# Dense backward of a four-layer attention stack: full-row band products, the feature map's derivative on VectorE, transposes moved behind the dh products

## The chip, the cores and the metric

The kernel runs on one core of one Trainium2 chip. The metric is the device time of one execution, in microseconds, as the median of several runs. Five engines take part: TensorE (PE in the profile, with PEld for its weight loads), VectorE (DVE), ScalarE (ACT), GpSimd (POOL) and SyncE (SP), which issues most of the transfers. Sixteen DMA engines move the data.

## The reference

Four residual layers run on 2048 rows of 640 numbers, 32 heads of 20 each. Layers 0 and 2 (kind A) are linear attention, layers 1 and 3 (kind B) are softmax attention in a sliding window of 256. The kernel computes the output and the gradients of the input and of the four weight matrices. The two parts that matter here are these:

```python
phi = lambda t: jnp.where(t > 0, t + 1, jnp.exp(t)) + 1e-6      # kind A
pq, pk = phi(q), phi(k)
kv = jnp.einsum("bhsd,bhse->bhde", pk, v)
z = jnp.einsum("bhsd->bhd", pk)
num = jnp.einsum("bhqd,bhde->bhqe", pq, kv)
den = jnp.einsum("bhqd,bhd->bhq", pq, z)[..., None] + 1e-6
o = num / den
...
x = x + _A_ref(_layernorm(x), A_wqkv, A_wo)      # layer 0, and again layer 2
x = x + _B_ref(_layernorm(x), B_wqkv, B_wo)      # layer 1, and again layer 3
```

The derivative of `phi` follows from its saved value: it is min(phi - 1e-6, 1). The kernel calls it `dphi`.

## The kernel before

The program does the forward pass, then for l = 3 and l = 1: the attention backward of layer l, and `seg_dense_bwd(l)`. The latter takes the gradient through the projection and the layer norm of layer l, and through the whole of layer a = l - 1 of kind A. It has two loops over 16 tiles of 128 rows. In loop 1 the gradient `dh` of the layer norm's output is the product of `dqkvT` (15 blocks of 128) with `WT`, in two halves of 320 columns (15 matmuls each, `dh0` and `dh1`). `ln_bwd` makes `car` of it, the gradient that flows on:

```python
def flip(self, src, n, dst, pt, eng, first=0):          # transposes on TensorE, up to 8 blocks per PSUM tile
    for i0 in range(0, n, 8):
        k = min(8, n - i0)
        tp = pt.tile([P, 1024], BF, name="t")
        for i in range(k):
            nc.tensor.transpose(tp[:, i * P:(i + 1) * P], src[:, c:c + P], self.ident)   # line 690
        (eng[(i0 // 8) % len(eng)])(dst[:, i0:i0 + k, :], v)                             # line 692

def ln_bwd(self, l, tt, ps, hn, g, pw):
    nc.scalar.activation(dhs, ps, ACT.Copy, scale=rs, accum_out=sm[:, 0:1])              # dh_s
    nc.vector.tensor_tensor_reduce(out=junk, in0=dhs, in1=hn, ..., accum_out=sm[:, 1:2]) # dh_junk
    nc.vector.tensor_scalar_mul(ab, sm, -1.0 / D)                                        # dh_ab
    nc.vector.scalar_tensor_tensor(out=u, in0=hn, scalar=ab[:, 1:2], in1=dhs, ...)       # dh_u
    nc.vector.scalar_tensor_tensor(out=self.car[:, tt, :], in0=u, scalar=ab[:, 0:1], in1=g, ...)
...
# seg_dense_bwd, loop 1
def flip_g(t):       # transposes car (5 blocks) into gT, copied by ScalarE; car is stored
def dO(t):
    p = self.do_mm(gT.pop(t), WoTA, pps)                     # 10 matmuls
    dN[t] = p1w.tile([P, 6 * P], BF, name="dN", bufs=3)
    s = self.do_scaled(a, t, p, o.pop(t), dN[t][:, 0:D], p1w)   # VectorE: dN; GpSimd: do_o; VectorE: do_s
    nc.gpsimd.memset(dN[t][:, D + H:], 0.0)
    nc.vector.tensor_copy(dN[t][:, D:D + H], s)
def flip_dN(t):      # transposes dN (6 blocks) into dNT, copied by ScalarE
def dq_band(t):
    for c in range(2):
        nc.tensor.matmul(p[:, c, 0:HD], lhsT=w[0:H, 5, :], rhs=mbdT[0:H, 5, ...])        # 32 rows, line 1075
        self.band_mm(p[:, c, 0:HD], w, mbdT, c, True)        # 3 narrow matmuls each, line 762
    ...                                                      # 10 matmuls into the bands, line 1083
    nc.gpsimd.tensor_scalar(out=f, in0=q, scalar1=-1e-6, scalar2=1.0, op0=ALU.add, op1=ALU.min)   # dphi
    nc.vector.tensor_tensor(out=dq[t], in0=p, in1=f, op=ALU.mult)
def flip_dq(t):      # transposes dq (5 blocks) into dqT, copied by ScalarE
plan = ((fetch, 2), (dh0, 0), (flip_g, -1), (flip_dN, -2), (dh1, 0), (dO, -1), (dq_band, -2), (flip_dq, -3))
for s in range(-2, TT + 3):
    for f, d in plan:
        if 0 <= s + d < TT:
            f(s + d)
```

The accumulators `d` of loop 1 rotate over two tiles of PSUM, the transposes `t` over two as well. Loop 2 has the same shape for the keys and values of layer a. `dkdv` makes two band products (with a one-row matmul of ones, line 1135) and multiplies the first by `dphi`; `flip_dkv` transposes 10 blocks, eight copied by ScalarE and two by VectorE; `dh0`/`dh1` and `ln_bwd` give the next `car`. Where a > 0 (so for l = 3 alone) `flip_g`, `dO` and `flip_dO` prepare the next attention backward. Its accumulators rotate over three tiles. An engine executes its instructions in order; the order between the steps of a loop is set by a scheduler when the program is built, from the order of the plan.

In the attention backward of layer 1 the weight gradients of layers 3 and 2 are filled in, so many pieces (a matmul or a load) per step; when they are done, the weights `WT`, `WoT` and `mbdT` of the dense part are put in the queue of loads, two per step, and the rest in one go at the end:

```python
self.seg_attention_bwd(l, it, lambda s: 11.9)     # 11.9 pieces per step
self.drain(it)
```

Of the kernel before, what the change touches and what calls it, by code (L numbers as in the profile page):

```python
# [12 lines left out]
ALU = mybir.AluOpType  # L13
# [3 lines left out]
P = 128  # L17
# [6 lines left out]
class Kern:  # L24
# [654 lines left out]
        self.dma(tile, dram, self.nc.sync)  # L679
        return tile  # L680

    def flip(self, src, n, dst, pt, eng, first=0):

        nc = self.nc
        for i0 in range(0, n, 8):
            k = min(8, n - i0)
            tp = pt.tile([P, 1024], BF, name="t")
            for i in range(k):
                c = (first + i0 + i) * P
                nc.tensor.transpose(tp[:, i * P:(i + 1) * P], src[:, c:c + P], self.ident)  # L690
            v = tp[:, 0:k * P].rearrange("p (i q) -> p i q", q=P)
            (eng[(i0 // 8) % len(eng)])(dst[:, i0:i0 + k, :], v)  # L692

    def do_mm(self, gT, WoT, pps):
        ps = pps.tile([P, 2, 512], F32, name="d")
# [30 lines left out]
        nc.vector.tensor_sub(sl[:, :, DH + 1], s, sl[:, :, DH])  # L726
        self.store(self.sv[l]["dO"][:, tt, :], dO)

    def dh_mm(self, ps, c, parts, WT):

        lhs = [t[:, k, :] for t, n in parts for k in range(n)]
        for k, w in enumerate(lhs):
            self.nc.tensor.matmul(ps[:, c, 0:self.HD], lhsT=w, rhs=WT[:, k, c * self.HD:(c + 1) * self.HD],  # L733
                                  start=(k == 0), stop=(k == len(lhs) - 1))

    def ln_bwd(self, l, tt, ps, hn, g, pw):
# [12 lines left out]
        nc.vector.scalar_tensor_tensor(out=u, in0=hn, scalar=ab[:, 1:2], in1=dhs, op0=ALU.mult, op1=ALU.add)  # L749
        nc.vector.scalar_tensor_tensor(out=self.car[:, tt, :], in0=u, scalar=ab[:, 0:1], in1=g,  # L750
                                       op0=ALU.add, op1=ALU.add)

    def dphi(self, p, pw):

        self.nc.gpsimd.tensor_scalar(out=p, in0=p, scalar1=-1e-6, scalar2=1.0, op0=ALU.add, op1=ALU.min)

    def band_mm(self, ps, lhsT, mat, c, seen):

# [254 lines left out]
    def seg_dense_bwd(self, l, w, mid):  # L1013
# [5 lines left out]
        with ExitStack() as st:  # L1019
# [7 lines left out]
            with ExitStack() as s2:  # L1027
                p1 = self.pool(s2, "b1")
                p1w = self.pool(s2, "b1w", 2)
                pl = self.pool(s2, "b1l", 3)  # L1030
                WTB, WoTA, mbdT = w
                WTA = WoTB = None
                pps = self.pool(s2, "ps", 2, PSUM)
                pbd = self.pool(s2, "psb", 1, PSUM)
                bands = [pbd.tile([P, 512], F32, name=f"band{i}") for i in range(2)]
                seen = [False, False]
                dT, hn, g, o, pq, ps, gT, dN, dNT, dq = ({} for _ in range(10))

# [12 lines left out]
                def dh1(t):  # L1051
                    self.dh_mm(ps[t], 1, [(dT.pop(t), self.QTT)], WTB)
                    self.ln_bwd(l, t, ps.pop(t), hn.pop(t), g.pop(t), pw)

                def flip_g(t):
                    gT[t] = pw.tile([P, DT, P], BF, name="gT")
                    self.flip(self.car[:, t, :], DT, gT[t], pt, [nc.scalar.copy])
                    self.dma(self.g_d[a][:, t, :], self.car[:, t, :], nc.gpsimd)

                def dO(t):  # L1060
                    p = self.do_mm(gT.pop(t), WoTA, pps)
                    dN[t] = p1w.tile([P, 6 * P], BF, name="dN", bufs=3)
                    s = self.do_scaled(a, t, p, o.pop(t), dN[t][:, 0:D], p1w)
                    nc.gpsimd.memset(dN[t][:, D + H:], 0.0)
                    nc.vector.tensor_copy(dN[t][:, D:D + H], s)

                def flip_dN(t):
                    dNT[t] = p1w.tile([P, 6, P], BF, name="dNT")
                    self.flip(dN[t], 6, dNT[t], pt, [nc.scalar.copy])

                def dq_band(t):
                    w = dNT.pop(t)
                    p = pps.tile([P, 2, 512], F32, name="d")
                    for c in range(2):
                        nc.tensor.matmul(p[:, c, 0:HD], lhsT=w[0:H, 5, :], rhs=mbdT[0:H, 5, c * HD:(c + 1) * HD],
                                         start=True, stop=False, skip_group_check=True)
                        self.band_mm(p[:, c, 0:HD], w, mbdT, c, True)
                    d, q = dN.pop(t), pq.pop(t)
                    for m in range(DT):
                        lo, hi = self.band[m]  # L1080
                        for off, r in ((self.boff[m], d[:, lo:hi]), (self.eoff[m], d[:, D:D + H])):
                            bank, c0 = off
                            nc.tensor.matmul(bands[bank][:, c0:c0 + r.shape[-1]], lhsT=q[:, m * P:(m + 1) * P], rhs=r,
                                             start=not seen[bank], stop=(t == TT - 1), skip_group_check=True)
                            seen[bank] = True
                    f = pw.tile([P, D], BF, name="dphi")
                    nc.gpsimd.tensor_scalar(out=f, in0=q, scalar1=-1e-6, scalar2=1.0, op0=ALU.add, op1=ALU.min)
                    dq[t] = p1w.tile([P, D], BF, name="dq_t")
                    nc.vector.tensor_tensor(out=dq[t].rearrange("p (c f) -> p c f", c=2), in0=p[:, :, 0:HD],
                                            in1=f.rearrange("p (c f) -> p c f", c=2), op=ALU.mult)  # L1090
                    self.dma(self.dqkv_d[a][:, t, 0:D], dq[t], nc.gpsimd)

                def flip_dq(t):
                    self.flip(dq.pop(t), DT, dqT[:, :, rows(t)], pt, [nc.scalar.copy])

                plan = ((fetch, 2), (dh0, 0), (flip_g, -1), (flip_dN, -2), (dh1, 0), (dO, -1), (dq_band, -2), (flip_dq, -3))
                for s in range(-2, TT + 3):
                    for f, d in plan:
                        if 0 <= s + d < TT:
                            f(s + d)  # L1100
                    self.drip(2)
                    if s == 2:
                        WTA = self.load_w(pb, 0, "WT")
                        WoTB = self.load_w(pb, 1, "WoT") if a > 0 else None
                dmbd, dmbdT = self.close_A_bwd(bands, pb, pt)
            mid()

            with ExitStack() as s2:
# [19 lines left out]

                def dkdv(t):
                    f = pw.tile([P, D], BF, name="dphi")  # L1130
                    nc.gpsimd.tensor_scalar(out=f, in0=pk.pop(t), scalar1=-1e-6, scalar2=1.0, op0=ALU.add, op1=ALU.min)
                    dkv[t] = p2w.tile([P, 2 * D], BF, name="dkv_t")
                    p = pps.tile([P, 2, 512], F32, name="d")
                    for c in range(2):
                        nc.tensor.matmul(p[:, c, 0:HD], lhsT=self.ones[0:1, :], rhs=dmbdT[0:1, 5, c * HD:(c + 1) * HD],
                                         start=True, stop=False, skip_group_check=True)
                        self.band_mm(p[:, c, 0:HD], vT[t], dmbdT, c, True)
                    nc.vector.tensor_tensor(out=dkv[t][:, 0:D].rearrange("p (c f) -> p c f", c=2), in0=p[:, :, 0:HD],
# [7 lines left out]

                def flip_dkv(t):
                    dkvT[t] = p2w.tile([P, 2 * DT, P], BF, name="dkvT")
                    self.flip(dkv.pop(t), 2 * DT, dkvT[t], pt, [nc.scalar.copy, nc.vector.tensor_copy])

                def dh0(t):
                    ps[t] = pps.tile([P, 2, 512], F32, name="d")
                    self.dh_mm(ps[t], 0, [(dqT[:, :, rows(t)], DT), (dkvT[t], 2 * DT)], WTA)

                def dh1(t):
                    self.dh_mm(ps[t], 1, [(dqT[:, :, rows(t)], DT), (dkvT.pop(t), 2 * DT)], WTA)
# [94 lines left out]
    def run(self):  # L1251
# [22 lines left out]
        for l in (3, 1):  # L1274
            with ExitStack() as s2:
# [89 lines left out]
```

The softmax here doesn't subtract the row's maximum and nothing guards it: scores larger than these inputs give would overflow.

## Time and profile before

| | |
|---|---|
| Time, median of 3 runs | 2542.8 us (2539.76 to 2553.88) |
| Span of the profiled run | 2552.5 us, mean granted TensorE clock 0.894 |
| Busy: PE, PEld | 2254.9 us (88%), 1452.3 us (57%) |
| Busy: DVE, ACT, POOL | 1436.1 us (56%), 1297.0 us (51%), 1096.6 us (43%) |
| Moved by DMA | 477.68 MB, mean 187 GB/s |
| Dense backward, l = 3: loop 1, loop 2 | about 1252 to 1394 us, 1410 to 1560 us |
| Attention backward, l = 1 | about 1580 to 2090 us |
| Dense backward, l = 1: loop 1, loop 2 | about 2116 to 2244 us (its first tiles from 2090), 2267 to 2366 us |
| Weight gradients at the end | 2366 to 2552 us |

A line of the timeline gives the start and the length of an instruction in us, the engine, the line of the program, the operation, and the tiles written and read. What stands in square brackets is the time for which the engine had been idle, and who released it. `x5` counts like instructions that follow one another and are shown as one. The bars of successive matmuls overlap, because matmuls are pipelined; the distance from one start to the next tells what a matmul really takes from the engine. A table of waits gives for a waiting engine and line, and for who ended the wait, the sum in us, the number of times, and the longest. A share of busy time is an average; the limit of a loop is found by following one tile of it through its engines.

### The profile page before, as it was taken

To read this page: it belongs to the slowest core of one execution; us is meant where nothing else is said; L and a number is where in the kernel's file an instruction comes from. 1 tells how busy PE (TensorE), PEld (TensorE's weight loads), DVE (VectorE), ACT (ScalarE), POOL (GpSimd) and SP (SyncE) were. 2 spreads that over 40 slices of the span, in tenths; PEclk is the share of its full clock that TensorE was granted. 3 is DMA by queue.
4 is the path that set the end of the run, shared out by engine and by line. 5 is a ranking of instruction groups with operands and counts; after the bars stand their busy time and mean duration, and the time that the engine had idled before them with its cause. 6 is when DMAs were issued, how large, how long until landed. Compare 5 with 4: busy or idle time off the path is not lost.

```text
span 2552.5 us, 69672 instructions
## 1 busy us (share of the span) xinstructions
PE 2254.9 (88%) x28242; PEld 1452.3 (57%) x28242; DVE 1436.1 (56%) x2651; ACT 1297.0 (51%) x2193; POOL 1096.6 (43%) x1584
## 2 busy tenths in 40 slices
PE   7888899888888799998898885989999988989989
PEld 5545565545555366666565663556666656656545
DVE  6645566556666467776565574555555545646212
ACT  5456677546666467777433443556656543334000
POOL 3445456545555434444465652223333335545000
PEclk9989999888999658786899997898999889979999
DMA  8589878678987798798784965979887879579687
GB/s 256 158 166 169 188 174 169 160 161 198 220 181 169 202 213 149 137 176 148 161 220 114 243 179 177 216 174 204 191 187 179 192 157 241 151 194 250 181 257 223
DMA packets 828306, 477.68 MB, mean 187 GB/s; under 512 B 573008, under 2 KB 806864, under 8 KB 827984
## 3 DMA queue, kind: packets, MB, share of 16 engines
q1 hardware_dynamic: 754640, 341.99, 62.6%
q0 software_dynamic: 24256, 84.57, 10.2%
q10 hardware_dynamic: 49088, 46.67, 5.8%
q8 instruction: 221, 3.62, 0.6%
q14 instruction: 101, 0.83, 0.1%
HBM read 190.35 MB, written 161.19 MB: 138 GB/s over the span
## 4 chain that ended last, share of the span: by engine, by line
PE 39%; DVE 8%; DMA 6%; ACT 4%; issue 4%; SPq 3%; POOL 0%; ACTq 0%; DVEq 0%; POOLq 0%
PE wg L1229 12%; PE acc L921 8%; PE sp L862 6%; PE d L733 5%; PE tp L906 4%; PE t L690 2%; DMA dsT<-ds 2%; SPq L125 2%; ACT e L876 2%; DVE car L750 2%; DVE dh_u L749 2%; DVE do_s L715 1%; DVE dh_junk L744 1%; ACT dh_s L741 1%; SPq L147 1%
## 5 line engine op out<-in xcount | busy, mean ns | idle before, releaser
L896 DVE SCALAR_TENSOR_TENSOR ds<-sp,e 128x768 bf16<-128x768 f32 (+2 forms) x512 | 463.5, 907 | 335.5 <-PE sp L862 238.5
L876 ACT ACTIVATE e<-sp 128x768 bf16<-128x768 f32 (+2 forms) x512 | 394.8, 774 | 203.2 <-PE sp L862 155.0
L399 ACT ACTIVATE e<-s 128x768 bf16<-128x768 f32 (+2 forms) x512 | 381.2, 772 | 195.7 <-PE s L397 147.6
L1229 PE MATMUL wg<-wg_r,wg_l 128*128 128x320 bf16 (+1 forms) x2240 | 408.5, 325 | 16.7 <-DMA out_dram<-wg_o 5.4
L880 POOL TENSOR_SCALAR_AFFINE_SELECT e<-e 128x512 bf16<-128x512 bf16 x256 | 162.5, 635 | 531.9 <-issue 410.7
L1229 PEld LDWEIGHTS <-wg_l 128*128 128x128 bf16 x2240 | 208.0, 99 | 137.7 <-issue 20.9
L404 POOL TENSOR_SCALAR_AFFINE_SELECT e<-e 128x512 bf16<-128x512 bf16 x256 | 162.9, 637 | 183.4 <-ACT e L399 180.1
L862 PE MATMUL sp<-KT,QT 32*128 32x384 bf16 (+2 forms) x1024 | 189.3, 366 | 38.7 <-ACT e L876 31.9
L353 PE MATMUL d<-W,ln_hnT 128*128 128x480 bf16 x640 | 178.4, 408 | 22.2 <-DMA ln_hnT<-ln_hn 12.9
L862 PE MATMUL sp<-VT,dOT 32*128 32x384 bf16 (+2 forms) x1024 | 191.5, 364 | 5.8 <-ACT e L876 4.8
L397 PE MATMUL s<-ring 32*128 32x128 bf16 x2880 | 169.8, 226 | 29.8 <-ACT e L399 23.6
L260 PE MATMUL d<-W,ln_hnT 128*128 128x320 bf16 x960 | 159.0, 315 | 11.8 <-ACT ln_hnT L692 6.5
L733 PE MATMUL d<-WT,dqkvT 128*128 128x320 bf16 x960 | 145.4, 306 | 15.8 <-DMA dqkvT<-dqkv 8.7
L397 PEld LDWEIGHTS <-ring 32*128 32x128 bf16 x2880 | 84.5, 95 | 124.1 <-issue 110.0
L906 PE MATMUL tp<-ident,ds 128*128 128x128 bf16 x1440 | 146.3, 245 | 6.3 <-DVE ds L896 5.7
L921 PEld LDWEIGHTS <-dsT 128*128 128x128 bf16 x2880 | 102.3, 99 | 87.0 <-issue 58.7
L921 PE MATMUL acc<-qk_r,dsT 128*128 128x40 bf16 (+1 forms) x2880 | 131.9, 183 | 22.0 <-DMA dsT<-ds 19.3
L407 POOL TENSOR_SCALAR_AFFINE_SELECT e<-e 128x512 bf16<-128x512 bf16 x224 | 144.4, 645 | 0.0
L884 POOL TENSOR_SCALAR_AFFINE_SELECT e<-e 128x512 bf16<-128x512 bf16 x224 | 142.1, 634 | 0.0
L744 DVE CUSTOM_DVE_ANT_0 dh_junk<-dh_s,hn_ld 128x640 bf16<-128x640 f32 x64 | 53.2, 832 | 157.5 <-ACT dh_s L741 133.4
L244 PE MATMUL d<-Wo,oT 128*128 128x320 bf16 x640 | 123.0, 323 | 18.1 <-DMA oT<-o_b 16.9
L944 ACT CAST dqkv_o<-acc 128x240 bf16<-128x240 f32 x256 | 91.7, 359 | 86.1 <-PE acc L921 61.2
(186 smaller groups left out, 4210.3 us busy)
## 6 DMA issues: line engine op xcount, KB each, us to landing
qkvT<-ring ACTq DMA_DIRECT2D x32, 768.0 KB, 5.0
dqkv<-dqkv_o POOLq DMA_DIRECT2D x32, 480.0 KB, 5.1
wg_r<-dqkv SPq DMA_DIRECT2D x96, 160.0 KB, 3.6
wg_r<-dqkv SPq DMA_DIRECT2D x64, 240.0 KB, 4.6
hn<-ln_hn SPq DMA_DIRECT2D x64, 160.0 KB, 2.8
qk<-qk_flat POOLq DMA_DIRECT2D x64, 160.0 KB, 4.4
qk_r<-qk SPq DMA_DIRECT2D x32, 320.0 KB, 4.6
hn_ld<-hn SPq DMA_DIRECT2D x64, 160.0 KB, 3.5
```

What stands on the lines that cost most here:

```text
L353: nc.tensor.matmul(ps, lhsT=hnT[:, k, :], rhs=W[:, k, ci * 480:(ci + 1) * 480], start=(k == 0), stop=(k == self.DT - 1))
L397: nc.tensor.matmul(ps[:, j, i * P:(i + 1) * P], lhsT=ring[r0:r0 + HP, G + g, kt * P:(kt + 1) * P], rhs=ring[r0:r0 + HP, g, qs], start=True ...
L399: nc.scalar.activation(ev[:, 2 * half:2 * half + 2], ps[:, :, 0:nkt * P].rearrange("p h (i q) -> p h i q", q=P), ACT.Exp, scale=self.c_att)
L404: nc.gpsimd.affine_select(out=ev[:, :, nkt - 1, :], in_=ev[:, :, nkt - 1, :], compare_op=ALU.is_ge, fill=0.0, base=0, pattern=[[0, 4], [1, ...
L733: self.nc.tensor.matmul(ps[:, c, 0:self.HD], lhsT=w, rhs=WT[:, k, c * self.HD:(c + 1) * self.HD], start=(k == 0), stop=(k == len(lhs) - 1))
L862: nc.tensor.matmul(ps[:, j, 0:nkt * P], lhsT=slabs[g][ta][r0:r0 + HP, b * P:(b + 1) * P], rhs=slabs[g][tb][r0:r0 + HP, k0 * P:(k0 + nkt) * P],
L876: nc.scalar.activation(ev[:, 2 * half:2 * half + 2], ps[:, :, 0:nkt * P].rearrange("p h (i k) -> p h i k", k=P), ACT.Exp, scale=c_att)
L880: nc.gpsimd.affine_select(out=ev[:, :, nkt - 1, :], in_=ev[:, :, nkt - 1, :], compare_op=ALU.is_ge, fill=0.0, base=0, pattern=[[0, 4], [-1 ...
L896: nc.vector.scalar_tensor_tensor(out=dv[:, hs], in0=ps[:, :, 0:nkt * P].rearrange("p h (i k) -> p h i k", k=P), scalar=c_att, in1=ev[:, hs ...
L906: nc.tensor.transpose(tp[:, i * P:(i + 1) * P], ds_of[u][:, (nb + i) * P:(nb + i + 1) * P], self.ident)
L921: nc.tensor.matmul(acc[:, hh * DH:hh * DH + w], lhsT=lhsT, rhs=rhs(rname, g, t, hh, w), start=(i == 0), stop=(i == len(s) - 1), skip_group ...
L1229: nc.tensor.matmul(ps, lhsT=lhs[:, tt, rows], rhs=rhs[:, tt, 0:w], start=(tt == 0), stop=(tt == TT - 1))
```

## The change

It has five parts, all in `seg_dense_bwd` but the last.

1. The matmuls on 32 rows and on one row of the band products become matmuls on all 128 rows. For that the tail of `dN` must be zero in columns that nothing writes: three fixed tiles `dNs`, cleared once, take the place of the pool's rotating tiles and of the memset per tile. `ones` and `dmbdT` have 128 rows already, with zeros beyond the first in the latter.
2. `dphi` moves from GpSimd to VectorE, in both loops.
3. In the plan of loop 1 the transposes of `car` and `dN` stand further behind in the row of `dh` matmuls (`dh1` is cut into its first nine matmuls and the other six), the transposes of `dq` stand ahead of the band products. In loop 2 `flip_dkv` and `flip_g` are moved likewise.
4. `flip_dkv` is split into five and five blocks, one half copied by ScalarE, the other by VectorE.
5. The weight gradients in the attention of layer 1 are filled in at 12.6 pieces per step.

```diff
-    def flip(self, src, n, dst, pt, eng, first=0):
+    def flip(self, src, n, dst, pt, eng, first=0, per=8):
-        for i0 in range(0, n, 8):
-            k = min(8, n - i0)
+        for i0 in range(0, n, per):
+            k = min(per, n - i0)
 ...
-    def dh_mm(self, ps, c, parts, WT):
+    def dh_mm(self, ps, c, parts, WT, first=0, end=99):
-        for k, w in enumerate(lhs):
+        for k, w in list(enumerate(lhs))[first:end]:
 ...                                                       # loop 1
+                dNs = [p1.tile([P, 6 * P], BF, name=f"dN{i}") for i in range(3)]
+                for x in dNs:
+                    nc.gpsimd.memset(x[:, D + H:], 0.0)
 ...
-                def dh1(t):
-                    self.dh_mm(ps[t], 1, [(dT.pop(t), self.QTT)], WTB)
+                def dh1a(t):
+                    self.dh_mm(ps[t], 1, [(dT[t], self.QTT)], WTB, 0, 9)
+
+                def dh1b(t):
+                    self.dh_mm(ps[t], 1, [(dT.pop(t), self.QTT)], WTB, 9)
                     self.ln_bwd(l, t, ps.pop(t), hn.pop(t), g.pop(t), pw)
 ...
-                    dN[t] = p1w.tile([P, 6 * P], BF, name="dN", bufs=3)
+                    dN[t] = dNs[t % 3]
                     s = self.do_scaled(a, t, p, o.pop(t), dN[t][:, 0:D], p1w)
-                    nc.gpsimd.memset(dN[t][:, D + H:], 0.0)
 ...
-                        nc.tensor.matmul(p[:, c, 0:HD], lhsT=w[0:H, 5, :], rhs=mbdT[0:H, 5, c * HD:(c + 1) * HD],
+                        nc.tensor.matmul(p[:, c, 0:HD], lhsT=w[:, 5, :], rhs=mbdT[:, 5, c * HD:(c + 1) * HD],
 ...
-                    nc.gpsimd.tensor_scalar(out=f, in0=q, scalar1=-1e-6, scalar2=1.0, op0=ALU.add, op1=ALU.min)
+                    nc.vector.tensor_scalar(out=f, in0=q, scalar1=-1e-6, scalar2=1.0, op0=ALU.add, op1=ALU.min)
 ...
-                plan = ((fetch, 2), (dh0, 0), (flip_g, -1), (flip_dN, -2), (dh1, 0), (dO, -1), (dq_band, -2), (flip_dq, -3))
+                plan = ((fetch, 2), (dh0, 0), (dh1a, 0), (flip_g, -1), (dh1b, 0), (flip_dN, -2), (dO, -1), (flip_dq, -3),
+                        (dq_band, -2))
 ...                                                       # loop 2
-                    nc.gpsimd.tensor_scalar(out=f, in0=pk.pop(t), ...)
+                    nc.vector.tensor_scalar(out=f, in0=pk.pop(t), ...)
-                        nc.tensor.matmul(p[:, c, 0:HD], lhsT=self.ones[0:1, :], rhs=dmbdT[0:1, 5, c * HD:(c + 1) * HD],
+                        nc.tensor.matmul(p[:, c, 0:HD], lhsT=self.ones, rhs=dmbdT[:, 5, c * HD:(c + 1) * HD],
 ...
-                    self.flip(dkv.pop(t), 2 * DT, dkvT[t], pt, [nc.scalar.copy, nc.vector.tensor_copy])
+                    self.flip(dkv.pop(t), 2 * DT, dkvT[t], pt, [nc.scalar.copy, nc.vector.tensor_copy], 0, DT)
 ...                                                       # dh1 becomes dh1a and dh1b as in loop 1
-                plan = ((fetch, 4), (fetch2, 2), (dh0, 0), *tail[:1], (flip_dkv, 1), (dh1, 0), *tail[1:2], (dkdv, 2),
-                        *tail[2:])
+                plan = ((fetch, 4), (fetch2, 2), (dh0, 0), (flip_dkv, 1), (dh1a, 0), *tail[:1], (dh1b, 0), *tail[1:2],
+                        (dkdv, 2), *tail[2:])
 ...
-                    self.seg_attention_bwd(l, it, lambda s: 11.9)
+                    self.seg_attention_bwd(l, it, lambda s: 12.6)
```

More of the change, by code (lines that the diff above doesn't have):

```diff
@@ L691, in flip @@
             v = tp[:, 0:k * P].rearrange("p (i q) -> p i q", q=P)
-            (eng[(i0 // 8) % len(eng)])(dst[:, i0:i0 + k, :], v)
+            (eng[(i0 // per) % len(eng)])(dst[:, i0:i0 + k, :], v)
     def do_mm(self, gT, WoT, pps):
@@ L751, in ln_bwd @@
                                        op0=ALU.add, op1=ALU.add)
-    def dphi(self, p, pw):
-        self.nc.gpsimd.tensor_scalar(out=p, in0=p, scalar1=-1e-6, scalar2=1.0, op0=ALU.add, op1=ALU.min)
     def band_mm(self, ps, lhsT, mat, c, seen):
@@ L1130, in dkdv @@
                     f = pw.tile([P, D], BF, name="dphi")
-                    nc.gpsimd.tensor_scalar(out=f, in0=pk.pop(t), scalar1=-1e-6, scalar2=1.0, op0=ALU.add, op1=ALU.min)
+                    nc.vector.tensor_scalar(out=f, in0=pk.pop(t), scalar1=-1e-6, scalar2=1.0, op0=ALU.add, op1=ALU.min)
                     dkv[t] = p2w.tile([P, 2 * D], BF, name="dkv_t")
@@ L1153, in dh0, with dh1a, dh1b @@
                     self.dh_mm(ps[t], 0, [(dqT[:, :, rows(t)], DT), (dkvT[t], 2 * DT)], WTA)
-                def dh1(t):
-                    self.dh_mm(ps[t], 1, [(dqT[:, :, rows(t)], DT), (dkvT.pop(t), 2 * DT)], WTA)
+                def dh1a(t):
+                    self.dh_mm(ps[t], 1, [(dqT[:, :, rows(t)], DT), (dkvT[t], 2 * DT)], WTA, 0, 9)
+                def dh1b(t):
+                    self.dh_mm(ps[t], 1, [(dqT[:, :, rows(t)], DT), (dkvT.pop(t), 2 * DT)], WTA, 9)
                     self.ln_bwd(a, t, ps.pop(t), hn.pop(t), self.car[:, t, :], pw)
```

## Prediction

> **What bounds the kernel now.** I first cut the span into stages with the table of busy time by stretch of time, because the page's averages mix stages with different limits. The change touches only the two dense backward segments (layers 3 and 1), each of two loops over 16 row tiles, and one number in the attention between them. The four loops, columns: stretch, length, busy time of PE, PEld, DVE, ACT, POOL, granted clock, DMA share, GB/s:
>
> ```profile
> 1252.00:1394.00 142.00, 128.28 (x1148) 88.89 (x1149) 84.33 (x140) 44.55 (x76) 81.62 (x78) 0.97 0.70 185
> ...
> 1410.00:1560.00 150.00, 131.15 (x1180) 91.79 (x1180) 101.50 (x186) 62.09 (x92) 79.67 (x76) 0.98 0.69 193
> ...
> 2116.00:2244.00 128.00, 117.73 (x1073) 82.09 (x1074) 76.65 (x129) 42.26 (x71) 71.80 (x72) 0.97 0.65 174
> ...
> 2267.00:2366.00 99.00, 95.48 (x826) 66.97 (x824) 61.00 (x105) 38.13 (x59) 53.72 (x43) 0.97 0.93 244
> ```
>
> Together they are 519 us of 2552; nothing else can give much. PE looks 88 to 96% busy, but a matmul's bar includes its pipelined end. So next the waits of PE (total us, times, longest), from 1252 to 1410 and from 1410 to 1580, that is loop 1 and loop 2 of layer 3:
>
> ```profile
> PE t L690 <- DVE car L750: 11.3, 15, 3.2
> ```
> ```profile
> PE t L690 <- DVE car L750: 17.8, 16, 4.5
> ```
>
> Once per tile PE stands still until VectorE has written `car`, which `flip_g` transposes. Therefore I read one tile of loop 1 in the timeline:
>
> ```profile
> 1341.38 0.30 PE L1075 MATMUL d<-mbdT,dNT 32*128 32x320 bf16 x1
> 1341.62 0.33 PE L762 MATMUL d<-mbdT,dNT 128*128 128x140 bf16 x3
> 1341.88 0.30 PE L1075 MATMUL d<-mbdT,dNT 32*128 32x320 bf16 x1
> 1342.12 0.33 PE L762 MATMUL d<-mbdT,dNT 128*128 128x80 bf16 x3
> ...
> 1343.38 1.45 DVE L749 SCALAR_TENSOR_TENSOR dh_u<-hn_ld,dh_ab,dh_s 128x640 f32<-128x640 bf16 x1
> 1344.75 0.81 DVE L715 TENSOR_REDUCE do_s<-do_o 128x32 f32<-128x640 f32 x1
> ...
> 1345.48 0.87 DVE L750 SCALAR_TENSOR_TENSOR car<-dh_u,dh_ab,g_ld 128x640 bf16<-128x640 f32 x1
> ...
> 1346.41 0.45 PE L690 MATMUL t<-ident,car 128*128 128x128 bf16 x5 [0.52 <-DVE car L750]
> ```
>
> Two things are to be seen. The 32-row matmul holds PE 0.24 us until the next starts (1341.38 to 1341.62), where ten full 320-column matmuls take 1.36 us in the chain, 0.136 each. And the loop is a ring: last `dh` matmul, `dh_s` on ScalarE, five to seven VectorE steps, `car`, `flip_g`, the remaining `dh` matmuls. The tiles repeat every 8.46 us (in the chain, 1313.34, 1321.80, 1330.27).
>
> **What the Trainium skill says.** *TensorEngine Tiling (Array Packing)*, Key Properties: changing the tiling mode drains TensorE. The trace agrees: 0.24 against 0.136 us, and after three 140-column matmuls (0.06 apart) about 0.08 us more is lost before the next 32-row one. *VectorE: DVE Perf Modes*, the perf-mode tier table: a bf16 `tensor_scalar` within SBUF runs four elements a cycle. The 128x320 one of line 274 takes 0.268 us in this trace; with 320 further elements at that rate and the page's 0.96 GHz, my estimate for the 128x640 `dphi` is 0.35 us, against 2.34 on POOL. *GPSIMD Engine Reference*, Specifications: POOL and VectorE share SBUF interfaces and contend when VectorE has two SBUF inputs. The trace agrees: `dh_u` takes 0.88 us alone and 1.45 beside `do_o`.
>
> **The change part by part.** The order in which the built kernels put instructions on each engine gives the new sequence. I set zero at the end of issue of the last `dh` matmul of a tile.
>
> *Loop 1* (both layers). Before: `flip_g` starts 6.48 after zero (1339.93 to 1346.41), then come 5 transposes (0.29), 6 transposes of dN (0.35) and 10 `dh` matmuls (1.36): 8.48, as measured. After: `flip_g` stands behind 24 `dh` matmuls, so only 0.29 and 6 x 0.136 = 0.82 follow it. The VectorE order becomes junk, `dh_ab`, `dN`, `dh_u`, `do_s`, `car`; the multiplication `dq_t` (0.82) moves behind `car`. That does not shorten the ring as one might hope, because `do_s` then waits for POOL's `do_o`. The last tile of loop 2 in layer 3 already has this order:
>
> ```profile
> 1554.02 0.82 DVE L707 TENSOR_TENSOR dO_t<-d,rinv 128x640 bf16<-128x640 f32 x1
> 1554.76 0.88 DVE L749 SCALAR_TENSOR_TENSOR dh_u<-hn_ld,dh_ab,dh_s 128x640 f32<-128x640 bf16 x1
> 1554.99 1.90 POOL L713 TENSOR_TENSOR do_o<-dO_t,o_ld 128x640 f32<-128x640 bf16 x1 [3.13 <-issue]
> 1556.92 0.82 DVE L715 TENSOR_REDUCE do_s<-do_o 128x32 f32<-128x640 f32 x1 [1.28 <-POOL do_o L713]
> 1557.66 0.88 DVE L750 SCALAR_TENSOR_TENSOR car<-dh_u,dh_ab,car 128x640 bf16<-128x640 f32 x1
> ```
>
> From junk (1553.08) to `flip_g` (1558.59) that is 5.51; junk starts 1.17 after zero (1339.93 to 1341.10). So `flip_g` at 6.68, the ring 6.68 + 0.29 + 0.82 = **7.79**. PE's own work: 8.46 less the wait of about 0.5, less 0.12 lost before the first 32-row matmul, less 2 x 0.2 for the full-row matmuls: 7.45. So the ring still bounds and the full-row matmuls bring nothing here. Gain 0.67 per tile. Only about 12.5 of 16 tiles run at 8.46 (the first ones take 7.9 and 8.2): 8.5 us per layer, **17 us**.
>
> *Loop 2, layer 3.* Before: `car` to `car` 1421.4 to 1541.2 over 13 tiles, 9.2 each; `flip_g` 6.8 after zero, and behind it 15 transposes and up to 11 `dh` matmuls. There `car` takes 1.20 where POOL's `dphi` starts beside it, 0.87 where it does not. After: ring = junk at 1.11, then start to start 0.75 (junk), 0.74 (`dO_t`), 0.07 (`dh_ab`), 0.73 (`dkv_t`), 1.43 (`dh_u`, still beside `do_o`), 0.73 (`do_s`), 0.93 (`car` and its signal): `flip_g` at 6.5. PE: `dO` 1.36, the two band products with full-row ones 0.17 + 0.17 + 0.31 + 2 x 0.136 = 0.92, `flip_dO` 0.45, 24 `dh` 3.26, `flip_dkv` 0.57: 6.56, then 1.10: **7.66**. Here PE and the ring meet, and the full-row ones (about 0.4 per tile) do count. `gT` on ScalarE ends too late by about 0.14 (`flip_g` to the next `dO` is 1.24 at 1551.07, against 1.10 of PE work): 7.8. The split by five costs VectorE 0.49 (128x640 from PSUM, line 196) for 0.28, and `dphi` 0.35; VectorE sums to about 6.9 of 7.8, so it is no bound. Gain 1.4 x 14 = **20 us**.
>
> *Loop 2, layer 1.* No `dO` and no ring: PE alone, 5.95 per tile. Two one-row matmuls become full: 0.4 x 16 = 6.4 us. But the DMA share is 0.93, in many slices of 6 us above 1, and PE waited 1.9 us for `vT`. I count half: **3 us**.
>
> *Pace 11.9 to 12.6.* The weight-gradient matmuls that fill the attention of layer 1 end some 8 steps sooner, so 20 of the 26 weight pieces, in place of 4, are issued before the last score transposes. Before, PE lost 2.4 us to a late transpose, 7.1 before the first `dh` and 3.0 at the third tile, where layer 3 waited 5.7 and lost nothing later. Gain about 2.4 + 1.4 + 3, less some 1.6 as 8 steps run without filling: **5 us**.
>
> *Memsets of dN* (0.2 us on POOL) and two others leave the path untouched: 0.
>
> Sum 17 + 20 + 3 + 5 = 45: 2542.8 - 45 = **2498 us**.
>
> **The rivals.** *Everything becomes PE-bound.* If `do_o` ran fast beside `dh_u`, loop 1 would fall to 7.45, 9 us more over both layers, and with all of loop 2 in layer 1: about 2486. Against it speaks the 1.28 wait for `do_o` above. *A new wait eats the reordering.* The sequence leaves little room: dN's PSUM copy (0.80) must end between the moved transposes and `dq_band`, behind `dh_s` on ScalarE; two accumulator buffers pass from hand to hand in loop 1. A wait of 0.4 in loops 1 and in loop 2 of layer 3 costs 0.4 x 44 = 18: about 2515. For it speaks that slacks I worked out are 0.05 to 0.2 us. *The transfers take over.* Faster loops raise the DMA share from 0.7 to about 0.8, so only layer 1's second loop is in danger: 3 us lost. *VectorE becomes the bound* through `dphi`: at 6.9 of 7.8 it would need 0.9 more per tile; if `dphi` ran at one element a cycle (0.8) it would just touch, without cost.
>
> **Range and chances.** The ring of loop 1 and the sum of loop 2 have each some 4 to 6 us of doubt, the pace 4, the DMA 3; together about 9, and the runs before spread by 14. Range 2484 to 2516. Two per cent is 2491.9, a gain of 51 against my 45: faster 0.32, same 0.66, slower 0.02.
>
> **What would show it.** Tiles 7.8 us apart in both loop 1s, with PE still waiting for `car` about 0.3 and `do_s` for `do_o`; 7.7 to 7.9 in loop 2 of layer 3 with hardly a wait for `car`; 5.55 to 5.8 in the last loop with more waits for `pkT` and `vT`; 0.136 from a band-ones matmul to the next; `dphi` on VectorE near 0.35 us; the first `dh` of layer 1 some 6 us after the attention's last matmul. I would be wrong if dN's copy or the accumulators stop PE, if `dphi` is far slower than 0.35, or if layer 1's attention itself grows longer with the denser filling.

## The result, and the profile after

The changed kernel takes 2504.9 us (median of 4 runs, 2500.3 to 2517.8), the kernel before 2541.3 (2538.8 to 2553.9). The ratio is 0.9855, 95% interval 0.9806 to 0.9904: 36 us less. The interval lies wholly below 1, and it ends just short of a gain of two per cent. The prediction was 2498, within 2484 to 2516.

To see where the time went, I divided both traces at the same events (first `dh` of loop 1, first `dh` matmul with `dqT` of loop 2, first score matmul, first weight-gradient matmul of the end):

| stage | before | after | difference | the prediction's term |
|---|---|---|---|---|
| all up to the first dense loop | 1253.0 | 1250.7 | -2.3 | 0 |
| loop 1, l = 3 | 157.6 | 148.8 | -8.8 | -8.5 |
| loop 2, l = 3 | 158.5 | 146.7 | -11.8 | -20 |
| attention, l = 1 | 529.7 | 523.2 | -6.5 | within the pace |
| loop 1, l = 1 | 165.9 | 151.5 | -14.4 | -8.5, and the pace's -5 |
| loop 2, l = 1 | 101.1 | 97.2 | -3.9 | -3 |
| weight gradients at the end | 186.7 | 186.0 | -0.7 | 0 |

The four loops together go from 583.1 to 544.2 us, 38.9 less. The rest of the difference between the two traces lies within what identical code spreads by from run to run (last section).

The busy time by stretch, for loop 1 and loop 2 of l = 3 and loop 2 of l = 1 (columns: stretch, length, PE, PEld, DVE, ACT, POOL, clock, DMA share, GB/s):

```profile
1250.00:1392.00 142.00, 127.95 (x1208) 94.24 (x1209) 90.46 (x181) 49.47 (x84) 50.72 (x49) 0.97 0.77 191
1399.00:1546.00 147.00, 128.71 (x1200) 95.39 (x1199) 101.75 (x205) 60.09 (x94) 49.10 (x63) 0.96 0.75 207
...
2221.00:2318.00 97.00, 91.41 (x834) 68.37 (x833) 61.87 (x119) 34.03 (x60) 15.83 (x29) 0.98 0.94 254
```

POOL fell from 81.6 to 50.7 us in the first stretch, 5% more matmuls fit into the same 142 us, and PE's share stayed where it was. The share doesn't tell whether PE bounds; the timeline does. One tile of loop 1 after (only the rows that the reading needs):

```profile
1319.86 0.88 DVE L749 SCALAR_TENSOR_TENSOR dh_u<-hn_ld,dh_ab,dh_s 128x640 f32<-128x640 bf16 x1
1320.01 3.42 PE L733 MATMUL d<-WT,dqkvT 128*128 128x320 bf16 x24
1320.08 1.91 POOL L713 TENSOR_TENSOR do_o<-dN,o_ld 128x640 f32<-128x640 bf16 x1 [2.57 <-issue]
1322.02 0.82 DVE L715 TENSOR_REDUCE do_s<-do_o 128x32 f32<-128x640 f32 x1 [1.29 <-POOL do_o L713]
1322.75 0.88 DVE L750 SCALAR_TENSOR_TENSOR car<-dh_u,dh_ab,g_ld 128x640 bf16<-128x640 f32 x1
...
1323.69 0.45 PE L690 MATMUL t<-ident,car 128*128 128x128 bf16 x5 [0.26 <-DVE car L750]
1323.98 0.98 PE L733 MATMUL d<-WT,dqkvT 128*128 128x320 bf16 x6
...
1324.48 0.33 DVE L1088 TENSOR_SCALAR dphi<-pq_ld 128x640 bf16<-128x640 bf16 x1
...
1326.77 0.30 PE L1076 MATMUL d<-mbdT,dNT 128*128 128x320 bf16 x1
1326.90 0.32 PE L758 MATMUL d<-mbdT,dNT 128*128 128x140 bf16 x3
```

To be seen: VectorE stands still 1.29 us for GpSimd's `do_o`; PE stands still 0.26 us for `car`, and 0.42 if one counts from starts (24 matmuls at 0.136 from 1320.01 on are issued by 1323.27, the transposes start at 1323.69); behind the transposes of `car` only 6 `dh` matmuls are left; and the full-row matmul holds PE for 0.13 us (1326.77 to 1326.90), where the 32-row one held it for 0.24. From `car` to `car` it is 7.78 us, tile after tile.

Where the gain fell short is loop 2 of l = 3. An ordinary tile on VectorE, and then one that comes at every fourth tile (both after):

```profile
1425.43 0.82 DVE L1140 TENSOR_TENSOR dkv_t<-d,dphi 128x640 bf16<-128x640 f32 x1
1426.16 1.44 DVE L749 SCALAR_TENSOR_TENSOR dh_u<-hn_ld,dh_ab,dh_s 128x640 f32<-128x640 bf16 x1
1427.53 0.81 DVE L715 TENSOR_REDUCE do_s<-do_o 128x32 f32<-128x640 f32 x1
1428.25 0.87 DVE L750 SCALAR_TENSOR_TENSOR car<-dh_u,dh_ab,car 128x640 bf16<-128x640 f32 x1
```
```profile
1457.25 0.88 DVE L749 SCALAR_TENSOR_TENSOR dh_u<-hn_ld,dh_ab,dh_s 128x640 f32<-128x640 bf16 x1
1459.41 0.82 DVE L715 TENSOR_REDUCE do_s<-do_o 128x32 f32<-128x640 f32 x1 [1.28 <-POOL do_o L713]
1460.15 0.88 DVE L750 SCALAR_TENSOR_TENSOR car<-dh_u,dh_ab,car 128x640 bf16<-128x640 f32 x1
...
1461.26 0.82 DVE L1140 TENSOR_TENSOR dkv_t<-d,dphi 128x640 bf16<-128x640 f32 x1
```

In the second, `dkv_t` is queued behind `car`: it starts 4.0 us after `dh_u`, not 0.7 ahead of it, so TensorE waits for it:

```profile
1460.10 0.57 PE L733 MATMUL d<-WT,dkvT 128*128 128x320 bf16 x3
1462.14 0.73 PE L690 MATMUL t<-ident,dkv_t 128*128 128x128 bf16 x10 [1.47 <-DVE dkv_t L1140]
```

The distances from `car` to `car` in this loop are 7.70, 7.82, 8.44, 9.71 and again: two tiles as predicted, two not.

### The profile page after: what moved, and what is told of

The parts are those of the page before. It is cut to its first block, busy times and chain, and to the rows that moved or that the text cites. A ratio compares the mean times of both kernels' runs of the same rounds, so it can differ in the third digit from the quotient of the medians.

```text
span 2504.1 us, 69571 instructions
## 1 busy us (share of the span) xinstructions
PE 2220.0 (89%) x28242; PEld 1456.1 (58%) x28242; DVE 1439.7 (57%) x2715; ACT 1288.0 (51%) x2193; POOL 950.9 (38%) x1494
## 4 chain that ended last, share of the span: by engine, by line
PE 40%; issue 6%; DMA 6%; DVE 4%; ACT 3%; SPq 3%; POOL 2%; ACTq 0%; DVEq 0%; POOLq 0%
PE wg L1234 13%; PE acc L917 9%; PE sp L858 7%; PE d L733 5%; PE tp L902 4%; POOL do_o L713 2%; SPq L125 2%; DMA dsT<-ds 2%; ACT e L872 2%; PE t L690 2%; DVE car L750 1%; SPq L147 1%; DVE ds L892 1%; DMA dqkvT<-dqkv 1%; PE d L698 1%
## 5 line engine op out<-in xcount | busy, mean ns | idle before, releaser
L1234 PE MATMUL wg<-wg_r,wg_l 128*128 128x320 bf16 (+1 forms) x2240 | 403.2, 323 | 19.7 <-DMA out_dram<-wg_o 5.5
L858 PE MATMUL sp<-KT,QT 32*128 32x384 bf16 (+2 forms) x1024 | 187.1, 362 | 31.5 <-ACT e L872 25.2
L902 PEld LDWEIGHTS <-ds 128*128 128x128 bf16 x1440 | 98.7, 108 | 50.6 <-issue 29.4
```

The source lines that it names most:

```text
L858: nc.tensor.matmul(ps[:, j, 0:nkt * P], lhsT=slabs[g][ta][r0:r0 + HP, b * P:(b + 1) * P], rhs=slabs[g][tb][r0:r0 + HP, k0 * P:(k0 + nkt) * P],
L902: nc.tensor.transpose(tp[:, i * P:(i + 1) * P], ds_of[u][:, (nb + i) * P:(nb + i + 1) * P], self.ident)
L1234: nc.tensor.matmul(ps, lhsT=lhs[:, tt, rows], rhs=rhs[:, tt, 0:w], start=(tt == 0), stop=(tt == TT - 1))
```

## The experiments

Whole runs of one kernel spread by 13 us and more here, so single edits can hardly be told by the total. The distances from one `car` to the next are far steadier: in loop 1 they repeat within 0.01 us from tile to tile and from kernel to kernel. So each experiment is read from these. Loop 1 and loop 2 of l = 1: median distance; loop 2 of l = 3, where the tiles differ: mean of 15 distances, good to about 0.1. The last column is the sum of the four loops in the trace, good to some 3 us (the first loads of a loop vary). One run each of E4 and E7 took 3792 and 3706 us, half as long again as all others, and is left out of the ratios.

| kernel | ratio to before, 95% interval | loop 1 | loop 2, l = 3 | loop 2, l = 1 | four loops |
|---|---|---|---|---|---|
| before | 1 | 8.46 | 9.08 | 5.95 | 583.1 |
| after | 0.9855 (0.9806 to 0.9904) | 7.78 | 8.23 | 5.82 | 544.2 |
| E1 narrow matmuls | 0.9889 (0.9839 to 0.9940) | 7.78 | 8.33 | 5.95 | 548.9 |
| E2 derivative on GpSimd | 0.9894 (0.9855 to 0.9932) | 7.78 | 8.38 | 5.82 | 547.3 |
| E3 old order | 1.0003 (0.9985 to 1.0022) | 8.51 | 8.84 | 5.82 | 572.1 |
| E4 split eight to two | 0.9895 (0.9849 to 0.9941) | 7.78 | 8.08 | 5.81 | 545.2 |
| E5 `do_s` behind `car` | 0.9883 (0.9835 to 0.9931) | 7.35 | 8.23 | 5.81 | 531.2 |
| E6 `flip_dkv` behind `dh` | 0.9881 (0.9835 to 0.9927) | 7.78 | 8.21 | 5.54 | 544.7 |
| E7 pace 11.9 | 0.9899 (0.9840 to 0.9959) | 7.78 | 8.14 | 5.82 | 547.8 |
| E8 three edits | 0.9815 (0.9777 to 0.9854) | 7.35 | 8.22 | 5.53 | 529.9 |
| E9 new order alone | 0.9908 (0.9877 to 0.9938) | 7.78 | 8.35 | 5.83 | 551.1 |
| E10 early band products | 0.9872 (0.9828 to 0.9915) | 7.78 | 7.80 | 5.82 | 542.8 |
| E11 E5 with narrow matmuls | one run | 7.77 | 8.43 | 5.95 | 543.7 |
| E12 best | 0.9791 (0.9755 to 0.9826) | 7.35 | 7.88 | 5.53 | 527.5 |

The tiles at the ends blur the column of loop 2 of l = 3: the first distance lies between 7.5 and 9.8, and in E10 and E12 two distances are only 6.4 and 6.5. Over one full period of four tiles in the middle the mean is 9.29 before, 8.42 after, 8.61 in E1 and in E2, 8.87 in E3, 8.15 in E4 and E8, 8.49 in E9, 8.03 in E10 and 8.05 in E12.

**Undoing one part.** E1 puts the narrow matmuls back, E2 the derivative on GpSimd, E3 the old order of both plans, E7 the old pace.

```diff
# E1
-  nc.tensor.matmul(p[:, c, 0:HD], lhsT=w[:, 5, :], rhs=mbdT[:, 5, ...])
+  nc.tensor.matmul(p[:, c, 0:HD], lhsT=w[0:H, 5, :], rhs=mbdT[0:H, 5, ...])
-  nc.tensor.matmul(p[:, c, 0:HD], lhsT=self.ones, rhs=dmbdT[:, 5, ...])
+  nc.tensor.matmul(p[:, c, 0:HD], lhsT=self.ones[0:1, :], rhs=dmbdT[0:1, 5, ...])
# E2, in both loops
-  nc.vector.tensor_scalar(out=f, ...)
+  nc.gpsimd.tensor_scalar(out=f, ...)
# E3: both plans as in the kernel before, dh1 still in two pieces
# E7
-  self.seg_attention_bwd(l, it, lambda s: 12.6)
+  self.seg_attention_bwd(l, it, lambda s: 11.9)
```

> The kernel after, but the matmuls that were made full-row are narrow again (32 rows in loop 1 of a dense layer, one row in loop 2). Theory (a ring through VectorE sets loop 1, so TensorE's time is hidden there; loop 2 is TensorE-bound): loop 1 stays within 0.15 us of 7.78 us per tile (+2 us per layer at most), loop 2 of l=1 goes from 5.82 to about 5.95 (+2 us), loop 2 of l=3 +3 to +5 us; the whole about +8 to +11 us, near 2515. Rival (TensorE bounds everywhere, so 0.4 us comes back in each of the 64 tile steps): +25 us, near 2530, loop 1 at 8.2 per tile. Rival (the waits around the drains swallow it): no difference, 2505.

Loop 1 doesn't move at all; loop 2 of l = 1 goes to 5.95, and in loop 2 of l = 3 the ordinary tiles go from 7.82 to 8.23, the whole 0.41 of the two narrow matmuls, while the two slow tiles of four (8.44, 9.71) stay. From its third `car` to its last that loop takes 109.7 us instead of 106.9. So full-row matmuls pay where TensorE bounds and nowhere else; the sizes are the theory's, a little less in loop 2 of l = 3.

> The kernel after, but the derivative of the feature map is computed on GpSimd again. Theory (it was off the path; what it costs is only GpSimd's collisions with VectorE): loop 1 stays at 7.8 to 8.1 us per tile, loop 2 of l=3 gains 0 to 4 us, the whole 0 to +8 us. Rival (moving the derivative was the main gain of the change, since GpSimd is nearly full): loop 1 above 8.3 per tile and the whole +15 us or more.

Loop 1 stays at 7.78, ordinary tiles of loop 2 of l = 3 rise from 7.82 to about 7.98. There, moving the derivative was worth 2 us or so. The rival falls. Loop 2 of l = 1 may hold another us or two: it takes 100.5 us in E2, 101.1 before and 99.5 in E9, the three kernels with the derivative on GpSimd, and 95.3 to 98.8 in the eleven others. In E2 TensorE waits 5.2 us there for `vT` and `pkT`, after 1.4 for `vT`. Why is not shown.

> The kernel after, but with the order of parts that the kernel before has (dN transposed ahead of dh, not behind it). Theory (the order is what shortened the ring of loop 1): loop 1 back to about 8.4 us per tile (+10 us per layer, +20 in all), loop 2 of l=3 to about 9 us per tile (+5 to +12 us); the whole near 2530. Rival (the order is neutral, the full-row matmuls and the derivative carried the gain): loop 1 within 0.15 of 7.78 and the whole within 5 us of the kernel after.

Without the new order the tile is 8.51 us, more than before, and the total is that of the kernel before, within 0.2%. The order carries loop 1. The four loops are 11 us shorter than before in E3's trace all the same, which the total doesn't show; the trace of before is that of a run 13 us above its median, and I leave open why. Of the 11 us, 5.0 lie in loop 1 of l = 1, whose first tiles jam in before (E7), and 2.5 in loop 2 of l = 1; E3 keeps the pace and the full-row matmuls that bear on these.

> The kernel after with the pace of the attention stage of l=1 at 11.9 again instead of 12.6. Theory (the pace only moves the point at which attention's fillers end): +5 to +12 us, all of it at the end of attention of l=1 and in the first tiles of loop 1 of l=1; the tile periods unchanged. Rival (the pace is neutral and the shorter attention in the trace after is spread between runs): within 2 us of the kernel after.

Loop 1 of l = 1 is 3.6 us longer (151.5 to 155.1). Alone that proves little, as it takes 154.5 in E1 at pace 12.6; the difference lies in the first tiles: the first two distances from `car` to `car` are 3.83 and 13.10 us, where they are 7.39 and 7.78 after. The same jam is in before (3.17 and 15.44) and in E9 (2.83 and 12.77), the other kernels with pace 11.9, and in no kernel with 12.6. E7's waits of TensorE there (engine, line, what for, total us, times, longest):

```profile
PE d L733 <- issue: 8.9, 1, 8.9
PE d L733 <- DMA dqkvT<-dqkv: 3.3, 2, 1.8
```

and in the kernel after, where one wait for the transposed `dqkvT` is followed by none:

```profile
PE d L733 <- DMA dqkvT<-dqkv: 6.6, 1, 6.6
```

From the first `dh` of this loop to its third `car` it is 29.3 us before, 29.0 in E7 and 26.9 in E9, and 22.7 to 25.2 in all kernels with 12.6 (23.8 after). So the pace is worth some 2 to 5 us, all at the start of this loop.

**One part alone.** E9 is the kernel before with nothing but the two new plans (and `dh1` in two pieces).

> The kernel before with one part of the change alone: the new order of the parts of both loops (with dh cut after nine of its matmuls). Narrow matmuls, derivative on GpSimd, the eight to two evacuation and pace 11.9 are as in the kernel before. Theory (the order carries most of the change): loop 1 at 7.8 us per tile instead of 8.46, loop 2 of l=3 at 8.3 to 8.6 instead of 9.1, loop 2 of l=1 at 5.95 as before; 10 us less per loop 1 and about 10 less in loop 2 of l=3, the whole 2512 to 2518 against 2541. Rival (the order pays only together with the derivative on VectorE and the full-row matmuls): loop 1 above 8.2, the whole above 2528.

The tiles of the first two loops are as expected (7.78; 8.35). Loop 2 of l = 1 is too uneven in this trace to tell: its median is 5.83 instead of 5.95, but its distances run from 4.07 to 9.31. The total is at the upper edge of what was expected: 0.9908 is 2518 us, some 23 of the change's 37 us. In the four loops it is 32.0 of 38.9. Together with E3: the order is most of the change.

**The ring of loop 1.** E5 takes the wait for `do_o` out of the ring by queueing `do_s` behind `car`; E11 is E5 with E1's narrow matmuls.

```diff
# in do_scaled, for loop 1
-  nc.vector.tensor_reduce(out=s, in_=self.hv(t), ...)
+  with self.tc.issue_after(car_of_the_next_tile):
+      nc.vector.tensor_reduce(out=s, in_=self.hv(t), ...)
```

> The kernel after, but in loop 1 of a dense layer the scaled dO (do_s) is queued on VectorE behind car instead of ahead of it, so that its wait for GpSimd's do_o no longer lies in the ring. Theory (loop 1 is bound by the ring dh, dh_s, VectorE, car, transposes of g, dh, in which VectorE waits 1.29 us for do_o): the tile goes from 7.78 us to TensorE's own 7.45 to 7.5, about 4.5 us less per layer, 9 us in all, near 2496. Rival (TensorE or another wait of equal length bounds it as well): stays at 7.7 to 7.8 and the whole within 2 us.

> The experiment with do_s behind car (loop 1 at 7.35 us per tile), and with the narrow matmuls put back. Theory (narrow matmuls cost TensorE about 0.4 us per tile, which loop 1 hid only because its ring was longer): without the long ring the cost shows, loop 1 goes from 7.35 to 7.7 to 7.78 us per tile. Rival (narrow matmuls cost nothing in loop 1 for another reason): it stays within 0.1 of 7.35.

E5 brings 7.35 us, 0.43 less per tile: the ring bound, and TensorE's own need is 7.35, not the 7.45 of the prediction. That is, within a hundredth, the 0.42 for which TensorE waited for `car` after. VectorE no longer waits for `do_o` (`dq_t` has moved into the gap), and TensorE waits for nothing in an ordinary tile:

```profile
1325.04 0.87 DVE L752 SCALAR_TENSOR_TENSOR dh_u<-hn_ld,dh_ab,dh_s 128x640 f32<-128x640 bf16 x1
...
1325.83 0.82 DVE L1093 TENSOR_TENSOR dq_t<-d,dphi 128x640 bf16<-128x640 f32 x1
1326.57 1.28 DVE L753 SCALAR_TENSOR_TENSOR car<-dh_u,dh_ab,g_ld 128x640 bf16<-128x640 f32 x1
...
1327.77 0.81 DVE L718 TENSOR_REDUCE do_s<-do_o 128x32 f32<-128x640 f32 x1
...
1328.45 0.44 PE L690 MATMUL t<-ident,car 128*128 128x128 bf16 x5
```

The first full-row matmul of the same tile (the lines of E5 are 3 further down than in the kernel after):

```profile
1324.16 0.30 PE L1079 MATMUL d<-mbdT,dNT 128*128 128x320 bf16 x1
1324.30 0.32 PE L761 MATMUL d<-mbdT,dNT 128*128 128x140 bf16 x3
```

and the same place in E11:

```profile
1324.93 0.30 PE L1079 MATMUL d<-mbdT,dNT 32*128 32x320 bf16 x1
1325.17 0.33 PE L761 MATMUL d<-mbdT,dNT 128*128 128x140 bf16 x3
```

From start to start that is 0.24 against 0.14. In front of the first one another 0.09 are lost (the transposes of dq start 0.37 ahead of it, in E5 0.28), and in front of the second 0.10; the tile is 7.77, 0.42 more. So the same matmuls that cost nothing in E1 cost 0.42 us as soon as the ring no longer covers them. That E1 shows exactly nothing is also luck: with narrow matmuls TensorE needs 7.77, the ring 7.78.

E5's four loops are 13 us shorter than those of after, but its total isn't (0.9883). In its trace the attention of l = 1, which the edit doesn't touch, takes 537.8 us against 523.2, at a granted clock of 0.91 against 0.93. Whether the edit has any part in that stays open; E8 and E12, which contain it, don't show so long an attention (531.2 and 527.6).

**Loop 2 of l = 3.** E4 undoes the split of the `dkvT` evacuation by five blocks; E10 keeps it and moves the band products forward.

```diff
# E4
-  self.flip(dkv.pop(t), 2 * DT, dkvT[t], pt, [nc.scalar.copy, nc.vector.tensor_copy], 0, DT)
+  self.flip(dkv.pop(t), 2 * DT, dkvT[t], pt, [nc.scalar.copy, nc.vector.tensor_copy])
# E10, a > 0; dk is the second half of dkdv
-  dh0, flip_dkv, dh1a, flip_g, dh1b, dO, dkdv, flip_dO
+  dh0, flip_dkv, dh1a, flip_g, dkdv, dh1b, dk, flip_dO, dO
```

> The kernel after, but the evacuation of the transposed dkv is split eight blocks to two again instead of five to five. Theory (the split by five is what puts VectorE's queue into another order at every fourth tile of loop 2 of l=3, which costs about 2.3 us each time): that loop goes to about 7.8 us per tile throughout, 7 us less than 146.7; loop 1 unchanged at 7.78; the whole about 2498. Rival (ScalarE's copy of eight blocks, about 1.0 us instead of 0.5, delays the next accumulator, so the split was a gain): that loop 146 us or longer, the whole 2505 or more.

Half of it: the slow tiles are gone (8.09, 8.14, 8.14, 8.23 and again), but the ordinary ones are no longer 7.82. In every tile TensorE now waits for VectorE's copy of `dkvT` before it can transpose `car`, 3.4 us in the first and 0.16 to 0.28 in the others. The waits of TensorE in this loop, E4:

```profile
PE t L690 <- DVE dkvT L692: 5.8, 14, 3.4
```

> The kernel after, with the order in loop 2 of l=3 changed once more: the first band product of dkdv goes between the two pieces of dh, the second behind dh, then the transposes of dO, then the matmuls of dO. The product dkv_t then runs on VectorE while VectorE would wait for dh_s, and never behind car. Theory (what is lost in that loop is VectorE's order alone, TensorE itself needs 7.8 us): all tiles at 7.6 to 7.8 us, the loop 6 to 8 us below 146.7, the whole about 2498. Rival (something else with a period of four tiles, such as the store of the transposed dO, holds it up): the pair of 8.44 and 9.71 us at every fourth tile stays. Rival (a new wait, for the accumulator that dO needs and dh_s has not yet read): every tile above 8.1 us.

Ordinary tiles are at 7.61 to 7.74: the theory of VectorE's order and TensorE's need holds for them. But the rival with the period of four holds too: every fourth distance is 9.15. The order of VectorE is now the same in all tiles, so this is another wait, the one of E4:

```profile
1447.16 0.71 PE L733 MATMUL d<-WT,dkvT 128*128 128x320 bf16 x4
1449.17 0.44 PE L690 MATMUL t<-ident,car 128*128 128x128 bf16 x5 [1.30 <-DVE dkvT L692]
```

So E10 gains little: 8.03 us in the mean of a period, and from the third `car` to the end of the loop 115.3 us instead of 117.9, where 6 to 8 less were expected. Its total (0.9872) shows no gain over after.

The transposes use two PSUM buffers in turn. In the program as built, the semaphore by which the transposes of `car` wait for their buffer is VectorE's in every tile of E4 and E9. In the kernel after and in E10 it is ScalarE's, except in every fourth tile, where it is VectorE's. In those tiles ScalarE's queue holds the issue of a store just ahead of its copy of `dkvT`; this is after:

```profile
1449.39 1.02 ACT L692 COPY dOT_ring<-t 128x1024 bf16<-128x1024 bf16 x1
1450.44 0.54 ACTq L125 DMA_DIRECT2D dOT<-dOT_ring  x1
1451.53 0.69 ACT L692 COPY dkvT<-t 128x640 bf16<-128x640 bf16 x1 [1.11 <-PE t L690]
```

So the split by five blocks has two sides. It gives the transposes of `car` a buffer that is free early, 0.32 us in an ordinary tile (8.14 to 7.82); but in the tile after each store the buffers swap, and with them VectorE's order, which costs 8.44 + 9.71 - 8.14 - 8.23 = 1.8 us per four tiles. Period means of 8.42 against 8.15 say that it isn't a gain as it stands. That the store causes the swap is inferred from its place; putting it on another queue wasn't tried.

**Loop 2 of l = 1.** After, 5.82 instead of my 5.55. One tile boundary of after on TensorE and ScalarE:

```profile
2266.60 0.48 PE L758 MATMUL d<-dmbd,pkT 128*128 128x140 bf16 x6
2267.20 0.84 PE L733 MATMUL d<-WT,dqT 128*128 128x320 bf16 x5
```
```profile
2266.26 0.79 ACT L741 ACTIVATE dh_s<-d,rs 128x640 f32<-128x640 f32 x1 [1.63 <-PE d L733]
```

Six band matmuls take 0.32 us to issue (2278.84 to 2279.16 in E6, below), here 0.60 go by. The next `dh` needs the accumulator that ScalarE's `dh_s` reads until 2267.05. E6 puts ten transposes in between.

```diff
# a == 0
-  dh0, flip_dkv, dh1a, dh1b, dkdv
+  dh0, dh1a, dh1b, flip_dkv, dkdv
```

> The kernel after, but in loop 2 of l=1 the transposes of dkv stand behind all of dh instead of in the middle of it. Theory (TensorE waits there about 0.3 us per tile for an accumulator that ScalarE's dh_s has not yet read, and the transposes can fill that time): the tile goes from 5.82 to about 5.55 us, 4 us less in all, near 2501. Rival (the weight transfers set that loop): stays at 5.8.

```profile
2278.84 0.48 PE L758 MATMUL d<-dmbd,pkT 128*128 128x140 bf16 x6
2279.16 0.84 PE L733 MATMUL d<-WT,dqT 128*128 128x320 bf16 x5
```

The distance is 5.54, as the theory has it, with the same transfers. The loop is 1.9 us shorter (97.2 to 95.3) instead of 4, which is hardly more than it varies by (96.5 to 98.8 in the other kernels with this order and the derivative on VectorE; 97.2 and 96.4 in E8 and E12, which have E6's edit). The distances at its start and around its eighth tile (8.04, after 7.87) did not shrink, and the last one grew from 4.07 to 5.18.

**Together.** E8 joins E4, E5 and E6; E12 joins E5, E6 and E10.

> The kernel after with three edits together: the scaled dO behind car in loop 1, the evacuation of dkv split eight to two in loop 2, and in loop 2 of l=1 the transposes of dkv behind dh. If all three theories hold: 9 + 7 + 4 us less, near 2485, loop 1 at 7.5, loop 2 of l=3 at 7.8, loop 2 of l=1 at 5.55 us per tile. If they share one limit: less than the largest alone.

> The kernel after with three edits: do_s behind car in loop 1, the early band products in loop 2 of l=3, and in loop 2 of l=1 the transposes of dkv behind dh. If all hold: loop 1 at 7.35 us per tile (7 us less per layer), loop 2 of l=3 at 7.6 to 7.8 (7 less), loop 2 of l=1 at 5.54 (2 less), together 21 to 23 us below the kernel after, near 2484.

The tile distances of loop 1 and of l = 1 add up in both. E4's tiles are in E8 as they were (8.15 in the mean of a period; a first distance of 9.76 makes the 8.22), 0.27 less than after. E12 has the lowest ratio: 2492.2 us, 0.9791 of before, with four loops 16.7 us shorter than after; its interval overlaps that of E8. It falls some 5 us short of its expectation, where E10 did: at every fourth tile of loop 2 (9.28).

## Why the prediction was right, and where it wasn't

- *The ring of loop 1, 8.48 to 7.79 per tile, 17 us:* right to 0.01 us (7.78) and in its cause. The 1.29 wait for `do_o`, found in one odd tile of the trace before, was there in every tile. From the third `car` to the sixteenth both loops shrank by 8.5 us (109.7 to 101.2). The claim that full-row matmuls bring nothing there is E1; that they would without the ring is E11.
- *Loop 2 of l = 3, 7.8 per tile, 20 us:* this step failed in size; it was 11.8, and the mean of a period 8.42. The term of 7.8 holds for half of the tiles. I read the order of instructions from a few tiles and multiplied by 14; two tiles of each four have another one, and cost 8.44 and 9.71. I counted the split by five as a cost of VectorE's time only (0.49 for 0.28) and didn't see that it decides which engine frees a PSUM buffer.
- *Loop 2 of l = 1, 3 us:* the size was near (3.9), but by luck, for the reason was wrong. Of the 0.40 us per tile only 0.13 came, some 2 us. Not transfers but the accumulator took back the rest: the time lost at the narrow matmuls had covered a wait for `dh_s`, and without them it shows (E6). The other 2 us of this trace lie within what the loop varies by, or come from the derivative (E2).
- *Pace, 5 us:* 5.5 at the start of loop 1 of l = 1 (29.3 to 23.8 us up to its third `car`), and 5.2 there when undone (E7). The wait of 3.0 us at the third tile is gone; that before the first `dh` is 6.6 us instead of 7.1, and the one for the late transpose 1.9 instead of 2.4. The 6.5 us less in the attention are not shown to be a gain of the change: see the last section.
- *The rivals:* "everything PE-bound" is refuted for loop 1 by E5. "A new wait eats the reordering" came true in part, in loop 2 alone and through another buffer than the ones I named. "Transfers take over" is refuted for the kernel after: E6 has 5.54 with the same transfers, and TensorE waits 1.4 us for loads in that loop, before 3.5, though the prediction looked for more. "VectorE the bound" is refuted by E5 and by the ordinary tiles of E10, which are shorter with the same work on VectorE. `dphi` on VectorE takes 0.33 us; the estimate from the Trainium skill's page *VectorE: DVE Perf Modes*, the perf-mode tier table, was 0.35. The 0.268 us that it started from is not what the trace before has for the 128x320 instruction of line 274: the median is 0.244 (0.187 to 1.098), and with that the same sum gives 0.33.

Sum: 8.8 + 11.8 + 14.4 + 3.9 = 38.9 us in the loops against 45 predicted. The 8 us missing in loop 2 of l = 3 are more than the whole miss; the other terms came out 2 us above their estimates. That the total lies within the range all the same is owed to the width of the range, 32 us.

## What to carry to other kernels

Before you price a faster instruction, find out what closes the cycle of the loop: 0.42 us per tile on TensorE were worth nothing inside a longer ring and all of 0.42 beside a shorter one. When two engines share the emptying of a rotating buffer, ask which of them frees the buffer that the next user gets, and look at a full period of the loop, not at one tile, before you multiply. A removed delay often covered another wait: look at what was going on behind it.

## What I had not expected of the hardware

The code up to the first dense loop is the same in all fourteen kernels of this study, yet it took 1240.2 to 1258.5 us in their traces, and the attention of l = 1 took 523.2 to 537.8 in the eleven with pace 12.6. The granted clock goes along by and large: in the attention it is 0.93 after (523 us), 0.92 in E1 (525) and 0.90 in E11 (532), but 0.91 in E5 (538). That spread is larger than most of the edits, while tile distances in loop 1 repeat to 0.01 us.

When `dh_u` on VectorE and `do_o` on GpSimd run side by side, the one that starts first keeps its time, and the later one pays. In the dense loops of after they overlap 45 times, and it was so each time: where `dh_u` starts first, if only by 0.2 us (as in the tile of loop 1 above), it takes 0.87 to 0.88 and `do_o` 1.90 to 1.95; where `do_o` starts first, it takes 1.39 to 1.47 and `dh_u` 1.44 to 2.05, as in the ordinary tile of loop 2 shown above, whose `do_o` is this:

```profile
1425.53 1.39 POOL L713 TENSOR_TENSOR do_o<-dO_t,o_ld 128x640 f32<-128x640 bf16 x1 [3.27 <-DVE dh_ab L747]
```

In E5 `dh_u` starts 0.22 ahead of `do_o` and takes 0.87, and `car`, which then starts while `do_o` is under way, takes 1.29 instead of 0.87. So which of them is charged is a matter of order. The prediction's "1.45 beside `do_o`" holds where `do_o` starts first, as in 43 of 44 overlaps before; after, `dh_u` starts first in 31 of 45. In loop 1 after, the bill thus goes to `do_o` (1.91 instead of 1.39), and from there into the wait of 1.29 us in front of `do_s`: some 0.5 of it, by my estimate from these two durations.
